# Rearranging the first fifteen microseconds of a fused attention and gated-MLP kernel: weight pieces, dummy matmuls, transposes and the place of block 3

## The chip, the cores and the metric

The kernel runs on one NeuronCore of a Trainium2 chip. The metric is the device time of one execution in microseconds; the kernel before took 1286.21 us (median of the five runs measured beside the change, 1286.20 to 1286.35).

## The reference, cut to what matters

```python
xn = layernorm(A_x)                                   # 2048 rows x 512
q  = xn @ wq ; p = softmax(q k^T / sqrt(128)) ; s = (p v) @ wo      # 32 heads
gate = xn @ W_gate ; up = xn @ W_up                   # 512 -> 1792 = 14 column blocks of 128
g  = silu((gate * (gate > 0) * up) @ W_down)
return x + s * g
```

The kernel starts with the gated MLP. Only its first part, for the first 512 rows (four tiles of 128), is touched.

## The kernel before

`pe`, `act`, `dve` and `sp` are TensorE, ScalarE, VectorE and the engine that issues most loads. `ps_r` is a ring of three slots of two PSUM banks each (gate, up); `ps_acc` is two more banks, used first by the transposes and later as accumulators. `FCS` cuts the weights' 14 column blocks into pieces that are loaded one after the other.

The loads, in order of issue:

```python
        FCS = [0, min(3, FC), min(8, FC), FC]
        HFC = 3
        ...
        warm_w = sem_ln1.sig(dve.memset(warm[:], 0.0))
        load_x0(sp, 0)
        load_x0(act, 1)
        load_w(sp, Wg_sb, wg_src, sem_wg, 0)
        load_w(act, Wu_sb, wu_src, sem_wu, 0)
        load_x0(sp, 2)
        load_x0(act, 3)
        load_w(sp, Wg_sb, wg_src, sem_wg, 1)
        load_w(sp, Wu_sb, wu_src, sem_wu, 1)
        if QB > 1:
            load_xq(1)
        load_w(sp, Wg_sb, wg_src, sem_wg, 2)
        load_w(sp, Wu_sb, wu_src, sem_wu, 2)
        for Q in range(2, QB):
            load_xq(Q)
        sem_wd.sig(sp.dma_start(Wd_sb[:], B_W_down.rearrange("(c p) d -> p c d", p=128)))
```

The head: per tile of 128 rows, statistics and centring on VectorE, four transposes on TensorE, a copy on ScalarE, then gate and up for column blocks 0 to 2. Each pair of a tile and a block is two groups of four matmuls of 128 columns (one group for gate, one for up), here called quartets. Dummy matmuls stand before it, because TensorE starts at half speed: in the profile of before the first dummies, 512 columns each, start 427 ns apart, and the matmuls of 512 columns of block 3 then 216 ns apart.

```python
        def head_center(n):
            atok = ln_aggr([n], ln_stats(n))
            _wait(dve, atok)
            return sem_ln4.sig(
                dve.tensor_scalar(xc_sb[:, n, :], x_sb[:, n, :], mv[:, n, 0:1], None, op0=ALU.subtract))

        def head_transpose(n, ntok):
            tp_ps = acc_bf[n % 2]
            _wait(pe, acc_free[n % 2])
            if n == 0:
                _wait(pe, tok_pool)
            _wait(pe, ntok)
            ins = None
            for c in range(DC):
                ins = pe.transpose(tp_ps[:, c * 128:(c + 1) * 128],
                                   xc_sb[:, n, c * 128:(c + 1) * 128], ident[:])
            ptok = sem_tp.sig(ins)
            src = tp_ps[:, 0:DC * 128].rearrange("p (c q) -> p c q", c=DC)
            _wait(act, ptok)
            acc_free[n % 2] = sem_xa.sig(act.copy(xcT[:, :, n * 128:(n + 1) * 128], src))
            return acc_free[n % 2]

        def warm_mm(k):
            for _i in range(k):
                pe.matmul(ps_r[:, 2 * NSLOT - 1, 0:D], warm[:, 0:128], warm[:], start=True, stop=True)

        def head_ln():
            ctok = {0: head_transpose(0, head_center(0))}
            warm_mm(2)
            for n in range(4):
                if n + 1 < 4:
                    ntok = head_center(n + 1)
                _wait(pe, ctok[n])
                head_tile(n, 0)
                if n + 1 < 4:
                    ctok[n + 1] = head_transpose(n + 1, ntok)
                for fc in range(1, HFC):
                    head_tile(n, fc)

        half_slots = []

        def head_tile(n, fc):
            hs = slice(n * 128, (n + 1) * 128)
            fs = slice(fc * 128, (fc + 1) * 128)
            if n == 0:
                half_slots.append(ring_acquire())
            s = half_slots[fc]
            for i, (W, sems) in enumerate(((Wg_sb, sem_wg), (Wu_sb, sem_wu))):
                if n == 0 and fc == 0:
                    pe.wait_ge(sems[0].h, 16)
                ins = None
                for c in range(DC):
                    ins = pe.matmul(ps_r[:, 2 * s + i, hs], W[:, c, fs], xcT[:, c, hs],
                                    start=(c == 0), stop=(c == DC - 1))
                if n == 3:
                    half_tok[(fc, i)] = (sem_gate if i == 0 else sem_gu).sig(ins)

        half_tok = {}

        ln_hold = {}

        ...
        _wait(pe, warm_w)
        warm_mm(10)
        head_ln()
```

After the head, blocks 3 to 13 follow for all 512 rows at once (matmuls of 512 columns); block n takes ring slot n mod 3, and has to wait until ScalarE's relu and VectorE's multiply have emptied it.

```python
        def finish_gate_up(Q, fc, s, gtok, gu_tok):
            par = Q % 2
            gb = 2 * s
            gk = fc % NSLOT
            _wait(act, gtok)
            _wait(act, gr_free[gk])
            rtok = sem_relu.sig(act.activation(gr_sb[gk][:], ps_r[:, gb, :], ACTF.Relu))
            _wait(dve, gu_tok)
            _wait(dve, rtok)
            if fc == 0:
                _wait(dve, hT_free[par])
            h_tok = sem_h.sig(
                dve.tensor_tensor(hT[par][:, fc, :], gr_sb[gk][:], ps_r[:, gb + 1, :], ALU.mult)
            )
            gr_free[gk] = h_tok
            ring_tok[s] = [rtok, h_tok]
        ...
                s = ring_acquire()
                gb = 2 * s
                if fc == 0:
                    _wait_all(pe, xt_ready[Q])
                xT, xs = (xcT, slice(0, NQ)) if Q == 0 else (xnT, qs)
                if Q == 0 and fc in FCS:
                    k = FCS.index(fc)
                    pe.wait_ge(sem_wg[k].h, 16)
                    pe.wait_ge(sem_wu[k].h, 16)
                ins = None
                for c in range(DC):
                    ins = pe.matmul(ps_r[:, gb, :], Wg_sb[:, c, fs], xT[:, c, xs],
                                    start=(c == 0), stop=(c == DC - 1))
                gtok = sem_gate.sig(ins)
                for c in range(DC):
                    ins = pe.matmul(ps_r[:, gb + 1, :], Wu_sb[:, c, fs], xT[:, c, xs],
                                    start=(c == 0), stop=(c == DC - 1))
                gu_tok = sem_gu.sig(ins)
```

The softmax here doesn't subtract the row's maximum and nothing guards it: scores larger than these inputs give would overflow.

## Time and profile before

| | before |
|---|---|
| median time, us | 1286.21 |
| profiled run, us (span 1284.5) | 1285.8 |
| PE busy, share of the span | 99% |
| first x landed (first statistics start) | 3.81 |
| first gate/up quartet | 6.32 |
| last head quartet / first matmul of block 3 in the trace | 12.14 / 13.15 |
| first gate/up of the second 512 rows | 44.02 |

Three lines of the page of the kernel before: TensorE's busy time, its granted clock in 40 slices, and the chain of work that ended last.

```profile
PE 1266.6 (99%) x11813; PEld 835.2 (65%) x12040; DVE 380.5 (30%) x685; ACT 1001.7 (78%) x1109; POOL 13.2 (1%) x25
...
PEclk9999999999999999999999999999999999999999
...
PE 85%; ACT 12%; issue 1%; DVE 1%; DMA 0%; DVEq 0%
```

TensorE is busy practically all the time and owns 85% of the chain; only its idle time counts. So the next view is the order of events at the start. The timeline of the kernel before, us from the start; columns are start, duration of the group, engine, line, operation, output<-inputs, shape, count, and in brackets the idle time before it and what ended it.

```profile
1.19 3.81 PE L369 MATMUL ps_r<-warm 128*128 128x512 bf16 x10 [1.19 <-DVE warm L234]
...
3.81 0.69 DVE L314 BATCH_NORM_STATS2 stats<-x_sb 128x6 f32<-128x512 bf16 x1 [2.68 <-DMA x_sb<-in_A_x_dram]
...
4.76 0.35 DVE L349 TENSOR_SCALAR xc_sb<-x_sb,mv 128x512 bf16<-128x512 bf16 x1
...
5.26 0.38 PE L359 MATMUL ps_acc<-ident,xc_sb 128*128 128x128 bf16 x4 [0.26 <-DVE xc_sb L349]
...
5.68 0.58 ACT L364 COPY xcT<-ps_acc 128x512 bf16<-128x512 bf16 x1 [1.99 <-PE ps_acc L359]
...
6.32 0.40 PE L397 MATMUL ps_r<-xcT,Wg_sb 128*128 128x128 bf16 x4 [0.24 <-ACT xcT L364]
...
6.55 0.39 PE L397 MATMUL ps_r<-xcT,Wu_sb 128*128 128x128 bf16 x4
...
6.78 0.39 PE L359 MATMUL ps_acc<-ident,xc_sb 128*128 128x128 bf16 x4
...
11.44 1.57 ACT L449 ACTIVATE gr_sb<-ps_r 128x512 bf16<-128x512 f32 x3 [0.53 <-PE ps_r L397]
...
12.14 0.39 PE L397 MATMUL ps_r<-xcT,Wu_sb 128*128 128x128 bf16 x4
12.15 0.69 DVE L455 TENSOR_TENSOR hT<-gr_sb,ps_r 128x512 bf16<-128x512 bf16 x1 [2.79 <-PE ps_r L397]
...
12.91 0.56 PEld L483 LDWEIGHTS ps_r<-xcT,Wg_sb 128*128 128x128 bf16 x4 [0.56 <-ACT gr_sb L449]
13.15 0.81 PE L483 MATMUL ps_r<-xcT,Wg_sb 128*128 128x512 bf16 x3 [0.63 <-ACT gr_sb L449]
...
13.80 1.03 PE L487 MATMUL ps_r<-xcT,Wu_sb 128*128 128x512 bf16 x4
...
19.22 0.69 DVE L314 BATCH_NORM_STATS2 stats<-x_sb 128x6 f32<-128x512 bf16 x1 [0.19 <-DMA x_sb<-in_A_x_dram]
```

The reader is to see four things. The ten dummies (first row) end at 5.0. The first x, through statistics, centring, transposes and copy, makes a chain from 3.81 to 6.32, and the copy is the named releaser of the first gate/up. The quartets then follow each other every 0.22 us: 6.32, 6.55, 6.78. And after the last one at 12.14 nothing starts until block 3, which waits behind a relu.

### The profile page before, as it was taken

Reading aid. Unit: us, or ns where it says so; the run is one execution under the profiler, and the core shown is the slowest. Engines: PE = TensorE matmul, PEld = TensorE weight load, DVE = VectorE, ACT = ScalarE, POOL = GpSimd, SP = SyncE. Lnnn points to the kernel's source line nnn. Section 1 sums busy time; section 2 is a strip of 40 time slices with the busy share of each in tenths; the row PEclk is TensorE's granted clock in tenths of the full one; section 3 lists DMA queues with packets and bytes.
Section 4 is the critical chain, followed back from the end, with each engine's and each line's share of the span. In section 5 each row is a group of like instructions: output and inputs, shape, how many; then the busy total and the mean of one; then the engine's idle time right before and its main releaser. Section 6 shows DMA issues by size and latency. Waiting matters only on the chain.

```text
span 1284.5 us, 26708 instructions
## 1 busy us (share of the span) xinstructions
PE 1266.6 (99%) x11813; PEld 835.2 (65%) x12040; DVE 380.5 (30%) x685; ACT 1001.7 (78%) x1109; POOL 13.2 (1%) x25
## 2 busy tenths in 40 slices
PE   9999999999999999999999999999999999999998
PEld 5444466676666666666666666666666666666665
DVE  6433311112222222222222222222222222224355
ACT  3322399998888888888888888888888888888884
POOL 2100000000000000000000000000000000000000
PEclk9999999999999999999999999999999999999999
DMA  9600123232222332332221322323323322332202
GB/s 263 131 1 1 22 47 55 60 56 37 36 54 46 71 54 50 55 70 51 54 45 32 67 46 54 55 67 55 55 51 70 54 36 38 51 67 55 49 15 75
DMA packets 240977, 72.13 MB, mean 56 GB/s; under 512 B 227808, under 2 KB 240864, under 8 KB 240864
## 3 DMA queue, kind: packets, MB, share of 16 engines
q1 hardware_dynamic: 240048, 69.76, 28.5%
q8 instruction: 96, 1.57, 0.5%
q10 hardware_dynamic: 816, 0.66, 0.2%
q14 instruction: 17, 0.14, 0.0%
HBM read 32.77 MB, written 2.10 MB: 27 GB/s over the span
## 4 chain that ended last, share of the span: by engine, by line
PE 85%; ACT 12%; issue 1%; DVE 1%; DMA 0%; DVEq 0%
PE ps_acc L737 32%; PE ps_r L640 25%; ACT PT L650 12%; PE ps_r L573 9%; PE ps_r L594 8%; PE ps_acc L506 4%; PE ps_r L487 4%; PE ps_r L483 4%; PE ps_r L774 1%; DVE fin_tmp L782 0%; PE ps_r L397 0%; DMA x_sb<-in_A_x_dram 0%; DVE x_sb L798 0%; ACT gr_sb L449 0%; PE ps_acc L359 0%
## 5 line engine op out<-in xcount | busy, mean ns | idle before, releaser
L650 ACT ACTIVATE PT<-ps_r 128x1024 bf16<-128x1024 f32 x1024 | 952.5, 1054 | 167.7 <-PE ps_r L640 164.9
L737 PE MATMUL ps_acc<-V_sb,PT 128*128 128x129 bf16 x8192 | 776.5, 220 | 10.7
L737 PEld LDWEIGHTS ps_acc<-V_sb,PT 128*128 128x128 bf16 x8192 | 621.1, 98 | 241.7 <-ACT PT L650 3.5
L640 PE MATMUL ps_r<-QT_sb,KT_sb 128*128 128x512 bf16 x1837 | 675.1, 379 | 0.3
L667 DVE RECIPROCAL rz_sb<-ps_acc 128x4 f32<-128x4 f32 x127 | 23.3, 183 | 729.8 <-PE ps_acc L737 729.8
L640 PEld LDWEIGHTS ps_r<-QT_sb,KT_sb 128*128 128x128 bf16 x2048 | 195.0, 98 | 1.1 <-DVE QT_sb L584 0.4
L573 PE MATMUL ps_r<-xnT,Wq_sb 128*128 128x512 bf16 x511 | 130.9, 379 | 0.1
L594 PE MATMUL ps_r<-Wo_sb,OT_store 128*128 128x512 bf16 x447 | 114.4, 379 | 0.1
L584 DVE CAST QT_sb<-ps_r 128x512 bf16<-128x512 f32 x128 | 88.5, 692 | 48.1 <-PE ps_r L573 48.1
L573 PEld LDWEIGHTS ps_r<-xnT,Wq_sb 128*128 128x128 bf16 x512 | 49.9, 97 | 60.6 <-ACT PT L650 27.1
L670 DVE TENSOR_TENSOR Onorm<-ps_acc,rz_sb 128x512 bf16<-128x512 f32 x127 | 87.8, 691 | 4.4
L594 PEld LDWEIGHTS ps_r<-Wo_sb,OT_store 128*128 128x128 bf16 x448 | 43.8, 98 | 52.9 <-ACT PT L650 0.2
L449 ACT ACTIVATE gr_sb<-ps_r 128x512 bf16<-128x512 f32 x56 | 32.9, 595 | 49.6 <-PE ps_r L483 49.1
L607 DVE TENSOR_TENSOR s_acc<-s_acc,ps_r 128x512 f32<-128x512 f32 x96 | 66.0, 687 | 17.4 <-PE ps_r L594 17.4
L455 DVE TENSOR_TENSOR hT<-gr_sb,ps_r 128x512 bf16<-128x512 bf16 x56 | 38.4, 685 | 46.8 <-PE ps_r L487 42.2
L506 PE MATMUL ps_acc<-Wd_sb,hT 128*128 128x512 bf16 x220 | 48.8, 379 | 0.2
L487 PE MATMUL ps_r<-xnT,Wu_sb 128*128 128x512 bf16 x164 | 42.7, 379 | 0.2
L483 PE MATMUL ps_r<-xnT,Wg_sb 128*128 128x512 bf16 x165 | 42.6, 379 | 0.2
L506 PEld LDWEIGHTS ps_acc<-Wd_sb,hT 128*128 128x128 bf16 x224 | 21.9, 98 | 26.4
L514 ACT ACTIVATE sig_sb<-ps_acc 128x512 f32<-128x512 f32 x12 | 7.2, 597 | 29.5 <-PE ps_acc L506 29.5
L487 PEld LDWEIGHTS ps_r<-xnT,Wu_sb 128*128 128x128 bf16 x168 | 16.4, 98 | 19.8
L483 PEld LDWEIGHTS ps_r<-xnT,Wg_sb 128*128 128x128 bf16 x168 | 16.4, 98 | 19.8
(50 smaller groups left out, 181.0 us busy)
## 6 DMA issues: line engine op xcount, KB each, us to landing
V_sb<-in_A_v_cache_dram SPq DMA_DIRECT2D x32, 512.0 KB, 4.8
Wq_sb<-in_A_wq_dram SPq DMA_DIRECT2D x32, 128.0 KB, 2.5
Wo_sb<-in_A_wo_dram SPq DMA_DIRECT2D x8, 512.0 KB, 4.9
OT_store<-Onorm SPq DMA_TRANSPOSE x127, 2.4
Wd_sb<-in_B_W_down_dram SPq DMA_DIRECT2D x1, 1792.0 KB, 14.6
x_sb<-in_A_x_dram SPq DMA_DIRECT2D x3, 512.0 KB, 12.1
out_dram<-x_sb SPq DMA_DIRECT2D x6, 256.0 KB, 2.2
Wg_sb<-in_B_W_gate_dram SPq DMA_DIRECT2D x1, 768.0 KB, 10.3
```

Source lines behind the costliest of these rows:

```text
L455: dve.tensor_tensor(hT[par][:, fc, :], gr_sb[gk][:], ps_r[:, gb + 1, :], ALU.mult)
L483: ins = pe.matmul(ps_r[:, gb, :], Wg_sb[:, c, fs], xT[:, c, xs], start=(c == 0), stop=(c == DC - 1))
L487: ins = pe.matmul(ps_r[:, gb + 1, :], Wu_sb[:, c, fs], xT[:, c, xs], start=(c == 0), stop=(c == DC - 1))
L506: ins = pe.matmul(ps_acc[:, jb, 0:D], hT[par][:, fc, j * 128:(j + 1) * 128], Wd_sb[:, fc, :], start=(fc == 0), stop=(fc == FC - 1))
L573: ins = pe.matmul(ps_r[:, bank, :], Wq_sb[b][:, c, :], xnT[:, c, qs], start=(c == 0), stop=(c == DC - 1))
L584: etok = sem_qpe.sig(dve.tensor_copy(QT_sb[b][:, qs], ps_r[:, bank, :]))
L594: ins = pe.matmul(ps_r[:, bank, 0:D], OT_store[g % 2][:, hh, n * 128:(n + 1) * 128], Wo_sb[g % 2][:, hh, :], start=(hh == 0), stop=(hh == ...
L607: dve.tensor_tensor(s_acc[:, n, :], s_acc[:, n, :], ps_r[:, bank, 0:D], ALU.add)
L640: ins = pe.matmul(ps_r[:, 2 * s + tt, :], KT_sb[h % 2][:, t * 128:(t + 1) * 128], QT_sb[h % 2][:, qs], start=True, stop=True)
L650: act.activation(PT[pb][:], ps_r[:, 2 * s:2 * s + 2, :], ACTF.Exp, scale=scale)
L670: dve.tensor_tensor(Onorm[ob][:], o_ap, rz_sb[:].to_broadcast([128, 4, Dh]), ALU.mult))
L737: ins = pe.matmul(o_ap, PT[pb][:, tt, j * 128:(j + 1) * 128], V_sb[vb][:, t, 0:VW], start=(t == 0 and j % 2 == 0), stop=(t == KT - 1 and j ...
```

## The change

The intent, step by step: (1) the first weights come in smaller pieces (2, 3, 4 and 5 blocks instead of 3, 5 and 6), the first gate and the first up piece on two queues as before, so that the first gate/up need not wait for them, and x of tile 3 leaves ScalarE's queue; (2) the dummies get 256 columns instead of 512 and a constant operand that VectorE need not write first, so they start earlier and block less; (3) the transposes of a tile stand ahead of the gate/up of the tile before it; (4) block 3 goes to the accumulator banks, so that it need not wait for ring slot 0. The diff, without context lines, and shortened where `...` or a comment says so:

```diff
@@ semaphores, loads @@
-        warm = S_([128, D], BF16, "warm")
-        sem_wg = [newsem(16) for _ in range(3)]
-        sem_wu = [newsem(16) for _ in range(3)]
+        sem_wg = [newsem(16) for _ in range(4)]
+        sem_wu = [newsem(16) for _ in range(4)]
-        FCS = [0, min(3, FC), min(8, FC), FC]
+        FCS = [0, 2, 5, 9, FC]
-        warm_w = sem_ln1.sig(dve.memset(warm[:], 0.0))
         load_x0(sp, 0)
         load_x0(act, 1)
         load_w(sp, Wg_sb, wg_src, sem_wg, 0)
         load_w(act, Wu_sb, wu_src, sem_wu, 0)
         load_x0(sp, 2)
-        load_x0(act, 3)
+        load_x0(sp, 3)
         load_w(sp, Wg_sb, wg_src, sem_wg, 1)
         load_w(sp, Wu_sb, wu_src, sem_wu, 1)
-        if QB > 1:
-            load_xq(1)
+        load_xq(1)
         load_w(sp, Wg_sb, wg_src, sem_wg, 2)
         load_w(sp, Wu_sb, wu_src, sem_wu, 2)
+        load_w(sp, Wg_sb, wg_src, sem_wg, 3)
+        load_w(sp, Wu_sb, wu_src, sem_wu, 3)
@@ dummies, head @@
+        ones_w = nc.const_aps.tensor(1.0, [128, 128], BF16)
+        ones_r = nc.const_aps.tensor(1.0, [128, 256], BF16)
         def warm_mm(k):
             for _i in range(k):
-                pe.matmul(ps_r[:, 2 * NSLOT - 1, 0:D], warm[:, 0:128], warm[:], start=True, stop=True)
+                pe.matmul(ps_r[:, 2 * NSLOT - 1, 0:256], ones_w, ones_r, start=True, stop=True)
         def head_ln():
-            ctok = {0: head_transpose(0, head_center(0))}
-            warm_mm(2)
-            for n in range(4):
-                ...
+            c0 = head_transpose(0, head_center(0))
+            warm_mm(4)
+            c1 = head_transpose(1, head_center(1))
+            n2 = head_center(2)
+            n3 = head_center(3)
+            _wait(pe, c0)
+            head_tile(0, 0)
+            head_tile(0, 1)
+            _wait(pe, c1)
+            head_tile(1, 0)
+            head_tile(1, 1)
+            c2 = head_transpose(2, n2)
+            head_tile(0, 2)
+            head_tile(1, 2)
+            _wait(pe, c2)
+            head_tile(2, 0)
+            c3 = head_transpose(3, n3)
+            head_tile(2, 1)
+            head_tile(2, 2)
+            _wait(pe, c3)
+            for fc in range(HFC):
+                head_tile(3, fc)
-                if n == 0 and fc == 0:
-                    pe.wait_ge(sems[0].h, 16)
+                if n == 0 and fc in FCS:
+                    pe.wait_ge(sems[FCS.index(fc)].h, 16)
-        _wait(pe, warm_w)
-        warm_mm(10)
+        warm_mm(18)
@@ block 3 @@
+        def gu_banks(s):
+            if s is None:
+                return ps_acc[:, 0, :], ps_acc[:, 1, :]
+            return ps_r[:, 2 * s, :], ps_r[:, 2 * s + 1, :]
-            ring_tok[s] = [rtok, h_tok]
+            if s is None:
+                y_bank_free[:] = [h_tok, h_tok]
+            else:
+                ring_tok[s] = [rtok, h_tok]
-                s = ring_acquire()
-                gb = 2 * s
+                if Q == 0 and fc == HFC:
+                    s = None
+                    _wait_all(pe, acc_free)
+                else:
+                    s = ring_acquire()
+                g_ps, u_ps = gu_banks(s)
 # ... the matmuls, relu and multiply take g_ps and u_ps in place of ps_r[:, gb, :] and ps_r[:, gb + 1, :]
```

More of the change, by code (lines that the diff above doesn't have):

```diff
@@ L365, in head_transpose @@
             return acc_free[n % 2]
+        ones_w = nc.const_aps.tensor(1.0, [128, 128], BF16)
+        ones_r = nc.const_aps.tensor(1.0, [128, 256], BF16)
         def warm_mm(k):
             for _i in range(k):
-                pe.matmul(ps_r[:, 2 * NSLOT - 1, 0:D], warm[:, 0:128], warm[:], start=True, stop=True)
+                pe.matmul(ps_r[:, 2 * NSLOT - 1, 0:256], ones_w, ones_r, start=True, stop=True)
         def head_ln():
-            ctok = {0: head_transpose(0, head_center(0))}
-            warm_mm(2)
-            for n in range(4):
-                if n + 1 < 4:
-                    ntok = head_center(n + 1)
-                _wait(pe, ctok[n])
-                head_tile(n, 0)
-                if n + 1 < 4:
-                    ctok[n + 1] = head_transpose(n + 1, ntok)
-                for fc in range(1, HFC):
-                    head_tile(n, fc)
+            c0 = head_transpose(0, head_center(0))
[20 more added lines that the diff above has]
+                head_tile(3, fc)
         half_slots = []
@@ L448, in finish_gate_up @@
             _wait(act, gr_free[gk])
-            rtok = sem_relu.sig(act.activation(gr_sb[gk][:], ps_r[:, gb, :], ACTF.Relu))
+            rtok = sem_relu.sig(act.activation(gr_sb[gk][:], g_ps, ACTF.Relu))
             _wait(dve, gu_tok)
@@ L454, in finish_gate_up @@
             h_tok = sem_h.sig(
-                dve.tensor_tensor(hT[par][:, fc, :], gr_sb[gk][:], ps_r[:, gb + 1, :], ALU.mult)
+                dve.tensor_tensor(hT[par][:, fc, :], gr_sb[gk][:], u_ps, ALU.mult)
             )
             gr_free[gk] = h_tok
-            ring_tok[s] = [rtok, h_tok]
+            if s is None:
+                y_bank_free[:] = [h_tok, h_tok]
+            else:
+                ring_tok[s] = [rtok, h_tok]
             if Q == 0:
@@ L471, in emit_gate_up @@
                     continue
-                s = ring_acquire()
-                gb = 2 * s
+                if Q == 0 and fc == HFC:
[3 more added lines that the diff above has]
+                    s = ring_acquire()
+                g_ps, u_ps = gu_banks(s)
                 if fc == 0:
@@ L482, in emit_gate_up @@
                 for c in range(DC):
-                    ins = pe.matmul(ps_r[:, gb, :], Wg_sb[:, c, fs], xT[:, c, xs],
+                    ins = pe.matmul(g_ps, Wg_sb[:, c, fs], xT[:, c, xs],
                                     start=(c == 0), stop=(c == DC - 1))
@@ L486, in emit_gate_up @@
                 for c in range(DC):
-                    ins = pe.matmul(ps_r[:, gb + 1, :], Wu_sb[:, c, fs], xT[:, c, xs],
+                    ins = pe.matmul(u_ps, Wu_sb[:, c, fs], xT[:, c, xs],
                                     start=(c == 0), stop=(c == DC - 1))
```

## The prediction

The text, made before the change was built or run:

> **What bounds the kernel now.** TensorE: the page gives PE 1266.6 of 1284.5 us busy (99%) at full clock; the chain of waits is 85% PE. The change touches only the first 15 us; later work only shifts. So: what does PE idle for in the front? The timeline shows:
> - to 1.19: VectorE's memset of the dummy operand;
> - 1.19 to 5.0: ten dummies, 427 ns apart, the last two faster;
> - 5.26: transposes of tile 0, behind x landing 3.79, statistics, aggregate, centring (to 5.11);
> - 6.32: first gate/up, released by ScalarE's copy (5.68 to 6.26), not by a weight (issue table: first gate weights land near 6.1, up 5.4);
> - to about 12.36: 24 gate/up quartets and 3 transpose quartets, 222 ns each, no gap;
> - 13.15: block 3, after 0.63 us idle by the page, some 0.79 us without a start; it waits for ring slot 0 (relus and multiply of block 0, done 12.84; the chain names the relus, ending 13.0).
>
> **What the change does.**
> 1. Block 3 goes to the accumulator banks, held only by the transposes' copies (free by about 11). The wait disappears: 0.7 to 0.8 us, on the critical path. Nearly the whole gain.
> 2. Transposes of tile 1 stand before the first gate/up. Centred tile 1 is ready at 6.32 and PE takes it some 0.14 later (as for tile 0), so the uninterrupted stretch starts near 6.46, not 6.32: cost 0.1 to 0.15. The quartets stay 27 x 222 ns = 6.0 us, and there was no wait among them to win.
> 3. Smaller first weights: their wait was not the last one, 0 us. Blocks 2 to 4 are needed near 8.7 to 8.9. From this trace's DMA rate (about 360 GB/s, 1.8 MB ahead, landing 0.7 us after the bytes by count) I estimate gate 7.2 to 7.6, up 8.3: just in time.
> 4. Dummies start near 0.9, without the memset: off the path, since x decides. 18 of 256 columns last 3.84 us when slow, end about 4.4 to 4.7 and leave 0.5 to 0.9 us idle before the transposes. The Trainium skill (TensorE: Matmul & The Clock Gate, Part 1) gives half clock until about 3.4 us of activity; this trace agrees: eight dummies at 427 ns are 3.41 us. A clock still slow at 6.4 would cost 1 to 3 us: a small risk.
> 5. Later PE runs 0.65 us further ahead of VectorE, which is full from 12.15 to 17.4 and waits for block 2's x at 19.22. Block 7 takes the slot of block 4 (multiply ends 19.03) at about 19.4, block 8 that of block 5 (20.8) at about 21.1: margins near 0.3. 1,024 more descriptors may delay the landing and eat 0 to 0.2 us.
>
> Sum: -0.75 + 0.13 + 0.05 = about -0.6 us, 0.05%.
>
> **Predicted: 1285.65 us**, 8 in 10 between 1285.0 and 1286.4. Faster by over 2%: 0.01. Within 2%: 0.98. Slower: 0.01.
>
> **What would show it.** Right: first block-3 matmul right behind the last head matmul, near 12.5 instead of 13.15; transposes of tile 1 before the first gate/up at about 6.46; no weight as a releaser of head matmuls; the same 0.6 us at the first down projection (32.09 before). Wrong: head quartets 427 ns apart (slow clock); a gap near 8.7 released by the second weights; idle PE at block 7 or 8 released by VectorE.
>
> **What would make it wrong.** x landing elsewhere than 3.79; a slow clock after the shorter dummies; late second weights; the gain given back at blocks 7 and 8, where the ring is tight.

## More of the kernel before

One row of the timeline of the kernel before, later on, is the mark for the sum of everything in the front: the first gate/up of the second 512 rows.

```profile
44.02 1.03 PE L483 MATMUL ps_r<-xnT,Wg_sb 128*128 128x512 bf16 x4
```

The profiled time minus this mark is 1241.78 us here.

## The result, and the profile after

Ratios are the mean time of one kernel's fast runs over that of the other's of the same rounds, so they are not quite the ratio of the medians quoted. The ratio here is 0.9997 with a 95% interval of 0.9983 to 1.0011: the same, at a threshold of 2%.

| | before | after |
|---|---|---|
| median time, us (5 runs each) | 1286.21 | 1285.83 |
| lowest and highest | 1286.20, 1286.35 | 1285.61, 1285.88 |
| profiled run, us | 1285.8 | 1285.83 |
| first x landed | 3.81 | 3.50 |
| start of the unbroken head (first quartet of gate/up before, of tile 1's transposes after) | 6.32 | 6.07 |
| first matmul of block 3 | 12.94 (by its weight load) | 12.95 |
| first gate/up of the second 512 rows | 44.02 | 44.07 |

The medians differ by 0.38 us, but the two profiled executions do not differ at all: the profile of before fell on one of that kernel's quicker runs (8 of the 37 told of next are as quick). This is why the kernel before was run again below. There are 37 runs of it, with a median of 1286.20 (1285.58 to 1287.25), against 10 runs of the kernel after with 1285.76 (1285.58 to 1285.88): a fall of 0.44 us. Ten of the 37 runs of before lie within the range of after, so single runs could not have shown it.

The lines of the page of the kernel after that answer to those of before:

```profile
PE 1278.6 (100%) x12050; PEld 836.3 (65%) x12050; DVE 380.6 (30%) x684; ACT 1001.5 (78%) x1109; POOL 13.3 (1%) x25
...
PEclk9999999999999999999999999999999999999999
...
PE 98%; DVE 1%; DMA 0%; SPq 0%; issue 0%; DVEq 0%
```

PE's busy time rose because more of its records arrived: before shows 11,813 matmuls beside 12,040 weight loads, after 12,050 beside 12,050. It says nothing about speed, and the different split of the chain (98% against 85%) is not read here for the same reason (after_again, the same kernel with 11,823 matmul records, shows 84%). The timeline of the kernel after, same columns as before:

```profile
0.77 3.68 PE L371 MATMUL ps_r<-const-bfloat16-1.0 128*128 128x256 bf16 x18 [0.77 <-PEq L900]
...
3.50 0.69 DVE L313 BATCH_NORM_STATS2 stats<-x_sb 128x6 f32<-128x512 bf16 x1 [3.50 <-DMA x_sb<-in_A_x_dram]
...
4.95 0.38 PE L358 MATMUL ps_acc<-ident,xc_sb 128*128 128x128 bf16 x4 [0.50 <-DVE xc_sb L348]
...
5.37 0.59 ACT L363 COPY xcT<-ps_acc 128x512 bf16<-128x512 bf16 x1 [2.21 <-PE ps_acc L358]
...
6.07 0.40 PE L358 MATMUL ps_acc<-ident,xc_sb 128*128 128x128 bf16 x4 [0.29 <-DVE xc_sb L348]
...
6.30 0.39 PE L410 MATMUL ps_r<-xcT,Wg_sb 128*128 128x128 bf16 x4
...
8.09 0.39 PE L358 MATMUL ps_acc<-ident,xc_sb 128*128 128x128 bf16 x4
...
8.31 0.39 PE L410 MATMUL ps_r<-xcT,Wg_sb 128*128 128x128 bf16 x4
...
9.36 0.40 PE L410 MATMUL ps_r<-xcT,Wu_sb 128*128 128x128 bf16 x4 [0.67 <-DMA Wu_sb<-in_B_W_up_dram]
...
12.72 0.39 PE L410 MATMUL ps_r<-xcT,Wu_sb 128*128 128x128 bf16 x4
...
12.95 1.03 PE L508 MATMUL ps_acc<-xcT,Wg_sb 128*128 128x512 bf16 x4
...
13.81 1.03 PE L512 MATMUL ps_acc<-xcT,Wu_sb 128*128 128x512 bf16 x4
...
19.66 0.69 DVE L313 BATCH_NORM_STATS2 stats<-x_sb 128x6 f32<-128x512 bf16 x1
```

The dummies now start at 0.77 and end at 4.45, half a microsecond before the transposes, which still run fast (0.38 us for four, as before). Block 3 follows the last head quartet, 12.72, by 0.23 us: its wait is gone. But there is a new hole: the gate quartet of tile 0 and block 2 starts at 8.31, its up quartet was due at 8.53 and starts at 9.36, released by the load of the up weights. These are the two landings, in the list of loads of the kernel after (KB, us from issue to landing; the issues stand at 2.67 and 3.15):

```profile
Wg_sb<-in_B_W_gate_dram SPq DMA_DIRECT2D x1, 384.0 KB, 5.5
Wu_sb<-in_B_W_up_dram SPq DMA_DIRECT2D x1, 384.0 KB, 6.2
```

The up piece thus landed near 9.3, where the prediction had estimated 8.3. The mark of the whole front in the kernel after:

```profile
44.07 1.03 PE L508 MATMUL ps_r<-xnT,Wg_sb 128*128 128x512 bf16 x4
```

It is 0.05 us later than in the profile of before, as the two profiled times say.

The page's totals of ScalarE and VectorE are unchanged (ACT 1001.5 against 1001.7 us, DVE 380.6 against 380.5), and so is the rest of the kernel.

### The profile page after: what moved, and what is told of

Same layout as the page of the kernel before. It is cut to its first block, busy times and chain, and to the rows that moved or that the text cites. A ratio compares the mean times of both kernels' runs of the same rounds, so it can differ in the third digit from the quotient of the medians.

```text
span 1284.5 us, 26955 instructions
## 1 busy us (share of the span) xinstructions
PE 1278.6 (100%) x12050; PEld 836.3 (65%) x12050; DVE 380.6 (30%) x684; ACT 1001.5 (78%) x1109; POOL 13.3 (1%) x25
## 4 chain that ended last, share of the span: by engine, by line
PE 98%; DVE 1%; DMA 0%; SPq 0%; issue 0%; DVEq 0%
PE ps_acc L761 36%; PE ps_r L664 34%; PE ps_r L597 9%; PE ps_r L618 8%; PE ps_acc L531 4%; PE ps_r L508 3%; PE ps_r L512 3%; PE ps_r L798 1%; DMA Wu_sb<-in_B_W_up_dram 0%; DVE fin_tmp L806 0%; PE ps_r L410 0%; DVE x_sb L822 0%; SPq L227 0%; PE ps_acc L512 0%; PE ps_acc L508 0%
## 5 line engine op out<-in xcount | busy, mean ns | idle before, releaser
L664 PE MATMUL ps_r<-QT_sb,KT_sb 128*128 128x512 bf16 x2048 | 754.1, 379 | 0.0
```

Of the source, the lines that this page charges most:

```text
L664: ins = pe.matmul(ps_r[:, 2 * s + tt, :], KT_sb[h % 2][:, t * 128:(t + 1) * 128], QT_sb[h % 2][:, qs], start=True, stop=True)
```

## The experiments

All ran for five rounds, four kernels to a call on one chip; each call has nine runs of the kernel before, with medians 1285.86 (first call), 1286.21 (second) and 1286.04 (third). That spread of 0.35 us for the same kernel is the yardstick; within the first call, too, the five runs of before_again have a median 0.35 us above the nine of the same kernel. A smaller difference between two medians is not read by itself. The 95% interval of every ratio contains 1 (for the fastest kernel, first3, it is 0.9981 to 1.0006). What follows therefore rests on the traces, on ranges that do not touch, and on runs put together over several calls.

| label | what it is | median | range | against the call's before |
|---|---|---|---|---|
| before_again | before | 1286.21 | 1285.80 to 1286.36 | +0.35 |
| after_again | after | 1285.65 | 1285.58 to 1285.83 | -0.21 |
| bank_only | before + block 3 in accumulators | 1285.72 | 1285.25 to 1285.79 | -0.14 |
| first3 | after with a three-block first piece | 1285.13 | 1285.02 to 1285.46 | -0.73 |
| bank_dum | before + accumulators + dummies | 1285.41 | 1285.25 to 1286.10 | -0.80 |
| dum_only | before + dummies | 1285.93 | 1285.63 to 1286.03 | -0.28 |
| first3_ring | first3, block 3 in the ring | 1285.85 | 1285.59 to 1286.09 | -0.36 |
| pieces_only | before + pieces | 1286.74 | 1286.70 to 1288.04 | +0.53 |
| order_only | before + order of the head | 1285.91 | 1285.58 to 1286.38 | -0.13 |
| up_act | after, second up piece on the other queue | 1286.06 | 1285.86 to 1286.25 | +0.02 |
| second2 | after with a two-block second piece | 1285.83 | 1285.50 to 1285.99 | -0.21 |
| first3_again | first3 once more | 1285.37 | 1285.06 to 1285.39 | -0.67 |

All were correct.

### before_again: the kernel before, unchanged

> The kernel before, unchanged, to see how far its front differs from run to run. Its profiled run lasted 1285.8 us, its timed runs 1286.2, and in that profile the first down projection starts at the same time as after the change (31.93 against 31.94 us). Theory 1 (the timed gain of 0.38 us is real and comes from the landing of the first x): the first statistics start near 3.8 to 4.2 us here, at least 0.3 later than the 3.50 seen after the change, and the time is 1286.2. Rival (run-to-run scatter of the landings): the first statistics move by 0.3 us between two profiles of the same kernel, and the times of this label scatter by 0.3 us or more.

Measured: 1286.21, with 1285.80 to 1286.36. The first statistics started at 3.59 instead of 3.81, and the mark at 44.28 instead of 44.02. Two rows of the timeline of this profile, the copy of tile 0 and the first gate/up:

```profile
5.46 0.59 ACT L364 COPY xcT<-ps_acc 128x512 bf16<-128x512 bf16 x1 [1.76 <-PE ps_acc L359]
...
6.60 0.38 PE L397 MATMUL ps_r<-xcT,Wg_sb 128*128 128x128 bf16 x4 [0.75 <-DMA Wg_sb<-in_B_W_gate_dram]
```

The copy ends near 6.05, so the quartet was due at 6.10. It starts at 6.60, held for 0.50 us by the first piece of the gate weights. In the first profile of before that piece had landed near 6.1, 0.2 us before it was needed. Theory 1, which wanted x at 3.8 or later, fails. The rival is right that the times scatter (by 0.56 us), though x moved by 0.22 us and not by its 0.3: the landing of x and of the weights moves from run to run by some tenths of a microsecond, and a three-block first piece is sometimes the last thing that arrives.

### after_again: the kernel after, unchanged

> The kernel after the change, unchanged. Theory 1: first statistics again at 3.5 us, the wait for the second piece of the up weights again about 0.7 us before 9.36, time 1285.8 (0.4 below the kernel before). Rival (scatter): landing of x and of the second piece each move by 0.3 us or more, and the time with them.

Measured: 1285.65 (1285.58 to 1285.83). x at 3.45, as theory 1 had it; the wait for the second up piece 0.36 us this time (0.83 in the first profile), as the rival had it. The mark stands at 43.89. Two new, small waits appear, because PE got ahead: block 8 starts 0.15 us late, and the first down projection loses 0.24. The row in the timeline of VectorE that starts it, the statistics of the second later block of x:

```profile
19.48 0.69 DVE L313 BATCH_NORM_STATS2 stats<-x_sb 128x6 f32<-128x512 bf16 x1 [0.40 <-DMA x_sb<-in_A_x_dram]
```

VectorE waited for that x until 19.48 (19.22 in before, where the wait was 0.2 and PE later), the multiply of block 5 moved back, and with it the slot that block 8 needs.

### bank_only: block 3 in the accumulators, nothing else

```diff
-                s = ring_acquire()
+                if Q == 0 and fc == HFC:
+                    s = None                      # ps_acc
+                    _wait_all(pe, acc_free)
+                else:
+                    s = ring_acquire()
```

> The kernel before with block 3 in the accumulator banks and nothing else. The trace of before is short of one matmul record of block 3; by its weight load the block starts at 12.91, so the wait is about 0.55 us from the last start's end at 12.36, not the 0.79 that the prediction used. Theory: block 3 starts right behind the head near 12.4, and the time falls by 0.5 to 0.6 us to about 1285.65 to 1285.7. If the prediction's size was right: 0.75, to 1285.45. Rival (the ring is tight behind block 3 and gives it back): PE idles at block 6, 7 or 8, the fall is under 0.3 us.

Measured: 1285.72, just above the theory's 1285.65 to 1285.70. Against all runs of before (1286.20) the fall is 0.48, against the nine of its call only 0.14, so the number alone does not rule out the rival. The trace does: block 3 follows the head without a gap, and no later block waits. This profile also shows the other accident of the front. Its timeline:

```profile
1.19 4.45 PE L369 MATMUL ps_r<-warm 128*128 128x512 bf16 x10 [1.19 <-DVE warm L234]
...
4.42 0.35 DVE L349 TENSOR_SCALAR xc_sb<-x_sb,mv 128x512 bf16<-128x512 bf16 x1
...
5.43 0.63 PE L359 MATMUL ps_acc<-ident,xc_sb 128*128 128x128 bf16 x4
...
5.85 1.06 PE L369 MATMUL ps_r<-warm 128*128 128x512 bf16 x2
...
6.74 0.47 PE L397 MATMUL ps_r<-xcT,Wg_sb 128*128 128x128 bf16 x4
```

Here the clock came up late: the ten dummies, at 427 ns each, last until 5.64. Tile 0 was centred by 4.77 (second row), but its transposes, in order behind the dummies, start at 5.43, and the next two dummies run slow too (1.06 us against 0.59 in before). The first gate/up starts at 6.74, though x had landed at 3.47, 0.34 earlier than in the first profile of before: 3.27 us after the landing, against 2.51 there. The same late start of the transposes, 5.43, stands in the profiles of pieces_only and order_only, so in three of five profiles with the long dummies.

### first3: a three-block first piece in the kernel after

```diff
-        FCS = [0, 2, 5, 9, FC]
+        FCS = [0, 3, 8, FC]
-        load_w(sp, Wg_sb, wg_src, sem_wg, 3)
-        load_w(sp, Wu_sb, wu_src, sem_wu, 3)
```

> The kernel after the change, but with the first piece of the weights three column blocks wide again (pieces of 3, 5 and 6 blocks); the order of loads and everything else as after. Theory 1 (the second piece is late and costs 0.83 us of PE time at 8.5 to 9.36): no gap there, block 3 starts near 12.1 to 12.2 instead of 12.95, time 0.7 to 0.85 us below after, about 1285.0 to 1285.1. Theory 2 (smaller first pieces are also what made x land 0.3 us earlier): x lands at 3.8 again, the gap is gone, and the fall is only 0.4 to 0.5, to 1285.35. Rival (the ring gives it back): no gap, but PE idles at blocks 7 or 8, time no better than 1285.7.

Measured: 1285.13 (1285.02 to 1285.46), 0.5 below after_again on the same chip, and the ranges do not touch. Matmul rows of its timeline:

```profile
6.13 0.40 PE L356 MATMUL ps_acc<-ident,xc_sb 128*128 128x128 bf16 x4 [0.29 <-DVE xc_sb L346]
6.37 0.39 PE L408 MATMUL ps_r<-xcT,Wg_sb 128*128 128x128 bf16 x4
...
11.95 0.39 PE L408 MATMUL ps_r<-xcT,Wu_sb 128*128 128x128 bf16 x4
12.39 0.81 PE L506 MATMUL ps_acc<-xcT,Wg_sb 128*128 128x512 bf16 x3
```

There is no hole at 8.5 and none before block 3 (its first record is missing again; counted back it starts at 12.17). x landed at 3.57, so theory 2, that the smaller pieces make x land early, has nothing for it; nor has the rival, since no later block waits. Taking the piece sizes of part (1) back more than doubles the gain over the kernel before (0.73 against 0.21 us): theory 1.

### bank_dum and dum_only: the accumulators with the dummies, and the dummies alone

```diff
-            warm_mm(2)          # 512 columns, operand from a memset
+            warm_mm(4)          # 256 columns, constant operand
-        warm_mm(10)
+        warm_mm(18)
```

> The kernel before with two parts of the change alone: block 3 in the accumulator banks, and the 256-column dummies (18 and 4) from the constant. Order of the head and pieces of the weights as before. Theory A (these two parts are the whole gain; the pieces cost, the reorder is worth nothing by itself): no gap at 8.5, block 3 begins right behind the head near 12.1 to 12.3, first down projection near 31.2, time 1285.1, as good as first3 (1285.13) and 0.5 below after (1285.65). Rival (the reorder is what lets the head run without a gap): 1285.5 or more, with idle PE among the head's matmuls that ScalarE's copies release.

Measured: 1285.41 (1285.25 to 1286.10), between the two expectations and 0.3 above what theory A gave. Block 3 follows the head without a gap and the mark is at 43.58. What is missing to 1285.1 is partly in the start of the head: in its profile x landed at 3.72, and the first gate/up was then held 0.2 us by the three-block gate piece (copy done near 6.18, start 6.41). Inside the head there is only one gap, of 0.07 us, before the transposes of tile 2, against the rival. So these two parts of the change make most of the gain that any layout gave (0.79 us below all runs of before; first3, the best, 1.02).

> The kernel before with the 256-column dummies alone. In the profile of bank_only the clock came up late: ten 512-column dummies ran until 5.63 and held up the transposes until 5.43, although the centred tile was ready near 4.8. Theory: the shorter dummies end by 4.6 at any clock, so the transposes never wait for them; the time is at the low end of the kernel before, 1285.7 to 1285.9, with less scatter above it (before: 1285.69 to 1287.25). Rival (the dummies do nothing but fill time): median 1286.0 to 1286.2 with the scatter of before. In both the wait of 0.57 us before block 3 stays.

Measured: 1285.93 (1285.63 to 1286.03), before in the same call 1286.21 (1285.58 to 1286.77). In its profile the clock was late again (four transposes take 0.58 us instead of 0.38), yet the transposes start at 4.85. So the mechanism is seen: the dummies no longer hold the transposes up. A slow clock still costs 0.2 us here, because the transposes themselves run slow: the first gate/up starts 2.71 us after x landed, against 2.51 in before and 3.27 in bank_only. The size, 0.28 us between medians, is below the yardstick; two of its five runs had a mean clock of 0.999 and were its two slowest. The wait before block 3 stays, 0.58 us.

### first3_ring: block 3 back in the ring

```diff
-                if Q == 0 and fc == HFC:
+                if False:
```

> first3 (the kernel after with a three-block first piece) with block 3 back in the ring. Theory: block 3 begins 0.55 to 0.6 us behind the head, released by ScalarE or VectorE, and the time is 0.55 above first3, near 1285.7. If the accumulators were worth the 0.75 of the prediction: 1285.9. If the reorder of the head already hid that wait: no difference to first3 (1285.13).

Measured: 1285.85, 0.72 above first3 of the other call and 0.48 above first3_again. In its own profile block 3 waits 0.58 us (last head quartet 12.18, due 12.40, start 12.98 by counting back), and a further 0.3 were lost at the first up weights, a scatter that the accumulators have no part in. By its time alone this run would suit the prediction's 0.75 us (1285.9) as well; the trace decides for 0.58. The wait of block 3 is 0.57 to 0.58 us in before, before_again, dum_only, first3_ring and order_only and 0.62 in pieces_only, all of which keep it in the ring.

### pieces_only: the smaller pieces alone

```diff
-        FCS = [0, min(3, FC), min(8, FC), FC]
+        FCS = [0, 2, 5, 9, FC]      # with a fourth semaphore, a wait at block 2, x of tile 3 on the other queue
```

> The kernel before with the weights in pieces of 2, 3, 4 and 5 blocks and x of tile 3 on the other queue, in the head order of before, which needs block 2 at about 7.6 instead of 8.3. Theory (the second piece lands at 8.8 to 9.3 and the pieces alone are a loss): PE idles for 1.0 to 1.7 us from about 7.6, released by the up weights; block 3 still waits 0.57 behind the head; time 1286.9 to 1287.6. Rival (the smaller first piece helps the start as much as the second costs): within 0.3 of before, 1285.9 to 1286.2.

Measured: 1286.74 (1286.70 to 1288.04), 0.53 above before: slower, but by half of what was expected. The hole in its head is 0.47 us (8.09 due, 8.56 start, released by the up weights), not 1.0 to 1.7: the piece landed at 8.5 here, and the late dummies had already moved the need for it from 7.6 to 8.1. So the pieces alone lose. The reorder of the head asks for block 2 only after ten quartets, not after five, and so probably makes them more bearable; no run has these two parts and nothing else.

### order_only: the order of the head alone

> The kernel before with the new order of the head alone (transposes of tile 1 ahead of the first gate/up, those of 2 and 3 ahead of the tiles before them); three-block first piece, long dummies and block 3 in the ring as before. Theory: by itself the reorder is worth nothing, since no matmul of the head waited for a transpose: time within 0.15 of the before on the same chip, wait of 0.57 us before block 3 unchanged. In runs whose first weights land late (6.5) it may hide 0.2 us, the transposes of tile 1, in that wait. Rival: it removes idle PE inside the head, 0.4 us or more faster.

Its diff is the new `head_ln` above, with two 512-column dummies. Measured: 1285.91 against 1286.04: -0.13, inside the theory's 0.15, and the wait before block 3 stays at 0.58. Its profile happens to be its slowest run (late clock, and the transposes of tile 2 waited for a late x). By itself the reorder is worth nothing that can be read here. Two rows of its timeline, the last head quartet and block 3:

```profile
12.73 0.39 PE L408 MATMUL ps_r<-xcT,Wu_sb 128*128 128x128 bf16 x4
13.54 1.02 PE L494 MATMUL ps_r<-xcT,Wg_sb 128*128 128x512 bf16 x4 [0.42 <-ACT gr_sb L460]
```

This trace lacks no matmul record (12,040 beside 12,040 weight loads), and block 3, due near 12.96, starts at 13.54. So the wait of 0.58 us stands without any counting back.

### up_act and second2: two ways to mend the second piece

```diff
 # up_act
         load_w(act, Wu_sb, wu_src, sem_wu, 0)
+        load_w(act, Wu_sb, wu_src, sem_wu, 1)
-        load_w(sp, Wu_sb, wu_src, sem_wu, 1)
 # second2
-        FCS = [0, 2, 5, 9, FC]
+        FCS = [0, 2, 4, 9, FC]
```

> The kernel after with the second piece of the up weights issued on ScalarE's queue, right behind the first, instead of on the sync queue behind four others. Theory (the bytes ahead decide, not the queue): the up piece lands earlier, near 8, but the gate piece and x of tiles 2 and 3 land later, since the engines are shared: PE still idles 0.3 to 0.9 us near 8.3, now released by the gate weights; time 1285.6 to 1285.9. Rival (the late landing is a matter of the queue): both pieces land before 8.3, no gap, time 1285.1 to 1285.2.

Measured: 1286.06, no better than before and 0.3 above the ten runs of the kernel after. The list of loads of up_act:

```profile
Wu_sb<-in_B_W_up_dram ACTq DMA_DIRECT2D x1, 384.0 KB, 6.4
Wg_sb<-in_B_W_gate_dram SPq DMA_DIRECT2D x1, 384.0 KB, 6.6
```

In after the gate piece took 5.5 us; beside an up piece on the other queue it takes 6.6. The up piece itself now lands near 8.1, but the gate quartet of block 2, due at 8.21, starts at 9.32, held by the gate weights (0.95 us idle by the page). Here the bytes ahead decide, not the queue. This is what the Trainium skill says (DMA: Bandwidth & Descriptors, section "Issuing engines are not separate DMA queues"): loads issued by several engines run on the same 16 DMA engines and interleave. This trace agrees.

> The kernel after with a second piece of two blocks instead of three (pieces of 2, 2, 5 and 5 blocks): 256 KB less ahead of its landing, by the rate of 350 GB/s 0.7 us earlier. Theory: the up piece lands near 8.2 to 8.6 against a need at 8.5, the gap near 8.3 shrinks to 0 to 0.15, and the first piece stays out of the way too: time 1285.0 to 1285.2, with block 3 near 12.1 to 12.3. Rival (the landing is late for another reason than the bytes): gap of 0.3 or more, 1285.5 or more.

Measured: 1285.83, not the 1285.0 to 1285.2 of the theory. The first half of the theory holds: the hole at 8.3 is gone and block 3 starts at 12.25, 0.7 earlier than in after. But the gain did not arrive. The timeline of second2 around block 8:

```profile
19.65 0.69 DVE L313 BATCH_NORM_STATS2 stats<-x_sb 128x6 f32<-128x512 bf16 x1 [0.72 <-DMA x_sb<-in_A_x_dram]
...
20.02 1.03 PE L512 MATMUL ps_r<-xcT,Wu_sb 128*128 128x512 bf16 x4
...
20.53 0.69 DVE L473 TENSOR_TENSOR hT<-gr_sb,ps_r 128x512 bf16<-128x512 bf16 x1
...
21.34 0.56 PEld L508 LDWEIGHTS ps_r<-xcT,Wg_sb 128*128 128x128 bf16 x4 [0.78 <-ACT gr_sb L467]
21.37 1.02 PE L508 MATMUL ps_r<-xcT,Wg_sb 128*128 128x512 bf16 x4 [0.32 <-DVE hT L473]
```

PE's last quartet of block 7 starts at 20.02, so block 8 was due at 20.89. It starts at 21.37, 0.48 late, because it takes the slot of block 5, whose multiply (20.53) stands behind statistics that waited for x until 19.65. In first3 the same statistics run at 18.81, with no wait in the profile. This x, the first load issued after all the gate and up weights, landed at 19.46 to 19.78 in the five profiles with small pieces and at 18.78 to 19.19 in the nine with three-block pieces, with the same bytes ahead of it. That is a second price of the small pieces. The pages show 1,056 more DMA packets for them (242,033 against 240,977), but no run tests whether the packets delay this x. Down the line the mark is at 44.06: of 0.7 us, 0.48 went at block 8 and 0.24 in the down projection. This is a miss of the expectation and the clearest view of point 5 of the prediction.

### first3_again: first3 beside second2

> first3 a second time, beside second2 on the same chip. In other kernels with a three-block first piece the first gate or up weights landed as late as 6.5 to 6.8 us and held the first gate/up by 0.2 to 0.7. Theory: times 1285.1 to 1285.5, at or slightly above second2. Rival (first3 is simply the better layout): 1285.1 and below second2.

Measured: 1285.37 (1285.06 to 1285.39), 0.46 below second2. The profile shows the theory's late weights: the first up quartet starts at 6.93 where 6.33 was due, held by the three-block up piece. Even so first3 is the better layout, and the rival's order is right, though not its 1285.1. Over its ten runs first3 has a median of 1285.18 (1285.02 to 1285.46): below every one of the ten runs of the kernel after and the 37 of before. It is the version that beats both.

## Why the prediction was right or wrong, point by point

The predicted time, 1285.65 us, with 1285.0 to 1286.4, holds the measured 1285.83; the predicted fall of 0.6 us was measured as 0.38, or 0.44 over all runs. That it came so near is partly luck. Block 3 was worth less than predicted (0.58 us), a wait for the second up piece that the prediction had at 0 took 0.36 and 0.83 us, and the dummies, which it held to be off the path, gave something back in runs with a late clock. Two profiles of the kernel after can be balanced against that of before, in us at the mark:

| term | predicted | after | after_again |
|---|---|---|---|
| first x lands earlier or later (scatter) | 0 | -0.31 | -0.36 |
| order of the head: from landing of x to the unbroken head | +0.13 | +0.06 | +0.05 |
| wait for the second up piece | 0 | +0.83 | +0.36 |
| wait before block 3 gone | -0.75 | -0.58 | -0.58 |
| wait before block 8 | 0 to +0.2 | 0 | +0.15 |
| wait within the first down projection | 0 | +0.04 | +0.24 |
| sum | -0.6 | +0.04 | -0.14 |
| read at the mark (44.02 before) | | +0.05 | -0.13 |

The sums close to within 0.01 us.

1. Block 3 ("The wait disappears: 0.7 to 0.8 us"). The mechanism is right: block 3 follows the head directly in every profile with the accumulators, and returns to its wait in first3_ring. The size is the term that was mis-sized: 0.58 us, read at 0.79. The step that failed is the reading: the first of four matmul records was missing, and the start of the second was taken for that of the block, one matmul of 0.216 us later. The count of three in the row and the weight load at 12.91 showed it, and order_only, whose trace is complete, has the same wait.
2. Order of the head: right, 0.05 to 0.06 us for a predicted 0.10 to 0.15, and nothing gained by itself (order_only).
3. Weights ("Smaller first weights: their wait was not the last one, 0 us"; "just in time"). Both halves fail, and the gap near 8.7 that the prediction named as a sign against itself is there. The second up piece landed at 8.8 to 9.3 instead of 8.3 and cost 0.36 and 0.83 us; the estimate took the 0.7 us between the bytes by count and the landing from the kernel before, and here it was 0.5 to 1.0 more. And the first piece was the last to arrive in four of the nine profiles with three blocks (before_again, bank_dum, first3_ring, first3_again), by 0.2 to 0.6 us; one trace had not shown it. The smaller pieces as a whole are a loss: first3, which takes them back, is 0.58 us faster than after in the medians of ten runs.
4. Dummies ("off the path, since x decides"). This fails for some runs: where the clock comes up late, the ten long dummies hold the transposes to 5.43, 0.5 us or more after the tile was centred. The feared risk, a clock still slow at the first gate/up, did not appear in any of the nine profiles with short dummies: apart from waits for weights their head quartets follow each other every 0.22 us. But in three of them (dum_only, up_act, second2) the clock was still slow a little earlier, and the four transposes took 0.58 us. Nor did the clock fall back in the gap: after the 0.5 us gap of the kernel after, four transposes took 0.38 us as before. The Trainium skill (TensorE: Matmul & The Clock Gate, Part 1) says that it takes an idle window of about 3.4 us to fall back; the trace agrees as far as it goes. When the clock rises is another matter: see the last section.
5. Blocks 7 and 8 ("margins near 0.3 us"; "eat 0 to 0.2 us"): right. It cost nothing in the first profile of after, where PE was too late for it, 0.15 in after_again, and 0.48 in second2, the kernel that brought PE there earliest with the small pieces. Not foreseen is the 0.24 us in the down projection that goes with it: VectorE, late, also delays the factor that the first tanh needs (it starts at 35.85 in after_again and 36.02 in second2, against 35.58 in before).

So where did the gain of 0.44 us over all runs come from? Against the median of all runs of before, 1286.20, the medians give a consistent, if rough, account: accumulators -0.48, dummies -0.27, both together -0.79, with the new order of head and loads -1.02 (first3, all runs), and the smaller pieces give back 0.58. Against the before of the same call alone the accumulators would have only -0.14, so of the single steps only the last is clear of the scatter, as are the sums of -0.79 and -1.02; the 0.58 us of block 3's wait rests on the traces and on first3_ring. That the second piece's wait is behind the 0.58 is shown (first3 removes it, second2 removes it and runs into block 8). That the dummies' part comes from runs with a late clock is seen in single profiles, and is not shown run by run, since there is one profile to a kernel. Whether the change moves the landing of the first x is open: 3.33 to 3.81 with the old long dummies, 3.31 to 3.72 with the new ones, without order.

## What to carry to other kernels

A smaller first piece of a load moves the wait to the second piece: count the bytes ahead of every piece that a tight stretch of work needs, add the lag from bytes to landing with room for its scatter, and try the uncut first piece as well. Before a wait is sized from one trace, check the instruction counts of its rows, and run the kernel before twice: here one trace had a missing record, first weights that were lucky to land in time, a clock that was lucky to rise early, and the latest first x of all fourteen profiles. When an engine is freed to run ahead, the next tight buffer behind it (here the ring at block 8) takes what the first one gave.

## What the Trainium skill lacked or had wrong

- TensorE: Matmul & The Clock Gate, Part 1, puts the rise to full clock "around 4µs into sustained matmul activity, ±500ns run-to-run". Here the spread is wider, and the rise can come earlier. The dummies of 512 columns first start 427 ns apart. In before_again the one at 3.72 is followed after 0.31 us, so the clock rose 2.5 to 2.8 us after the first dummy at 1.19. In before the one at 4.15 is followed after 0.26 us: 3.0 to 3.2 us, so only seven dummies were slow for their whole length, and the 3.4 us that the prediction took over do not fit. In bank_only the dummies, back to back from 1.19 to 5.64, never sped up, and the two after the transposes (5.85) still took 1.06 us instead of 0.59: slow for at least 4.7 us. The ±500 ns do not allow that spread; the page's remark in the same Part that one kernel had 6, 11 or 14 slow matmuls in different runs fits better.
- DMA: Bandwidth & Descriptors has a fit for a single DMA ("Anatomy of one DMA": about 2.0 us plus the bytes, on the gpsimd path) but we found nothing on how late a load of a deep queue lands behind its share of the bytes. In these traces a 384 KB piece landed 5.6 to 6.2 us after its issue with 1.4 MB ahead of it (the second up piece of after_again and after), and the same piece moved between two executions of the same kernel by 0.5 us (landed at 9.3 and 8.8).
- The page Perfetto Trace Analysis does not say that single matmul records can be missing from a profile. In before, PE has 11,813 matmul records beside 12,040 weight loads (nine of the fourteen profiles lack 227, the other five none), block 3's first quartet shows three of four, and this one record changed a wait from 0.58 to 0.79 us.
